# Attention, a Fourier mixer and a gated block on one core: the last row in half-width pairs, the accumulators read ahead of a residual add, the last copies shared otherwise, and a new written order

## The chip, the cores and the metric

The kernel runs on one core of a Trainium2 chip. The core has a matrix engine (TensorE, PE in the rows), a vector engine (VectorE, DVE), an activation engine (ScalarE, ACT), a general engine (GpSimd, POOL), and an engine that issues transfers (SyncE, SP). Each works through its own queue in the order in which its instructions were written; they meet at semaphores. The metric is the time of one execution on the device in microseconds, lower is better.

## The reference

Three stages follow one another. All is float32, with batch 2, 768 positions and 512 channels (8 heads of 64).

```
for each block of 64 positions:                     # decayed linear attention
    out   = ((q k^T) * Dmask) v + (q * lam^(i+1)) state
    state = lam^64 * state + (k * lam^(63-i))^T v
u  = x + real(fft2(x))                              # x: attention output, fft over 768 positions and 512 channels
un = (u - mean(u)) / sqrt(var(u) + 1e-6)
x  = u + relu(un @ w_ch1) @ w_ch2                   # w_ch1 512x2048, w_ch2 2048x512
gate = sigmoid(causal conv of 5 taps over x)
out  = (gate * (x @ w_val)) @ w_out
```

## The kernel before, in words

**Stages.** Each batch element has six chunks of 128 positions for the attention. A chunk `(b, c)` is loaded by `L` (four transfers on SP), gets its scores by `S` (two halves), the mask product on VectorE by `s`, the product with v by `A`, the part from the state by `E`, and the next state by `T` and `t`; `k` and `Kq` scale k and q, `a` and `e` copy the output out of PSUM. `X` moves half of the channels by one partition with transfers on SP. The Fourier stage folds the sequence (`Xm`, `Xe`, `Xo`, `Xx`), transforms the channels (`XD`, with the table cd) and then the positions (`XQ` with the sine table, `XP` with the cosine table), and adds the result into U (`Xc`, `Xq`, `Xp`, `Xu`). Channel 256 of the transform stands alone in one row: `XK` (`fft_P256`, L405) computes it, `XF` (`fft_fix`, L410) puts it into row 0 of the tiles mp. `XA` (`fft_a384`, L335) makes the values that stand for the middle position, for the rows and for channel 256. The step names with a number in front, `0` or `1`, mean the batch.

**Blocks.** After that come four blocks of 384 positions. `Nm` to `Np` are the layer norm; `F` is the first product (16 slices of the hidden width), `f` and `h` its relu as a high and a low part; `G k,f,d` adds slice f into accumulator d (four PSUM banks); `U`, `u`, `V`, `v` split weights into a high and a low part (three products per matmul, `mm3`, L618). In block 0 the first product takes the weights whole. The weights arrive as 64-bit words, and `Dl`, `Da`, `Db`, `Dc`, `De`, `Dx` load and convert them, mostly beside block 0. At a block's end `Rm` (L662) multiplies an accumulator by the reciprocal deviation, and `R` (L666, through `gadd`, L500) adds it to U; `Ha` (L659) gives the next block its four accumulators, which are the same banks, so the first `G` of the next block into bank d waits for `Rm` of d. `M...` is the gated block, one block behind; in the last block `Ev` and `Eo` do its products and `Es` (`end_store`, L686, through `m_store`, L761) copies three tiles of 128 positions out of PSUM and stores them.

**Order.** Nothing is planned at run time: one list, ORDER (L59 to L109), names 1446 steps, and each step is written in that order into its engines' queues. For steps in `GPS` a plus sign behind the step means VectorE and no plus GpSimd; for those in `ACTS` a plus means VectorE and no plus ScalarE. A step that stands later in the list can still run earlier than one on another engine; on one engine the list's order is kept. PSUM tiles with one tag share banks: `pso2` has two, `ph` two, `acc0` to `acc3` one each. U tiles, tables and accumulators are guarded by semaphores that the framework places.

Of the kernel before, what the change touches and what calls it, by code (L numbers as in the profile page):

```python
# [906 lines left out]
```

## Time and profile before

| what | value |
|---|---|
| median of three runs | 451.94 us (450.45 to 452.24) |
| profiled execution, its own time | 451.17 us |
| its span on the core | 449.4 us |
| TensorE busy, share of the span | 438.9 us, 98% |
| VectorE busy | 313.5 us, 70% |
| ScalarE busy | 243.6 us, 54% |
| GpSimd busy | 128.3 us, 29% |
| granted TensorE clock | 1.00 |
| DMA packets | 40.45 MB, mean 90 GB/s |

Busy time is the time in which an engine had at least one instruction at work; matmuls are pipelined, so their ends overlap the next start, and the pace is read from one start to the next. A float32 matmul makes two records in the trace. A row of the timeline gives the start, the time taken, the engine (PEld is the weight load), the line of the kernel, the operation, what it writes and reads, and how many instructions are merged in it; a bracket gives the idle time before it and what ended it.

### The profile page before, as it was taken

How to read it: one execution, taken by the hardware profiler on the slowest of the kernel's cores; microseconds unless marked ns; L12 is line 12 of the kernel's file. 1: busy time of each engine (PE TensorE's matmuls, PEld its weight loads, DVE VectorE, ACT ScalarE, POOL GpSimd, SP SyncE). 2: the span in 40 equal slices, each digit the busy share in tenths (PEclk: the TensorE clock that was granted, in tenths of full speed). 3: DMA queues.
4: the chain of work that ended last, by engine and by line, in shares of the span. 5: the costliest groups of instructions: out<-in, count | busy, mean ns of one | idle time of the engine just before them, and what ended most of it. 6: DMA issues, size and time to landing. Idle time of an engine off the chain costs nothing.

```text
span 449.4 us, 7061 instructions
## 1 busy us (share of the span) xinstructions
PE 438.9 (98%) x2738; PEld 391.8 (87%) x2738; DVE 313.5 (70%) x498; ACT 243.6 (54%) x496; POOL 128.3 (29%) x114
## 2 busy tenths in 40 slices
PE   7999999999999999899999999999999999999996
PEld 6788767678677779899999999999999999999994
DVE  5768789999999998876756478614645893331594
ACT  5454666767767665585426456434634753341442
POOL 1132224101230112343362547232514512330230
PEclk9999999999999999999999999999999999999999
DMA  7999953647733610000000000000000010000101
GB/s 265 327 321 272 393 184 114 207 182 264 269 105 122 224 50 1 1 2 0 1 0 25 0 1 23 1 1 25 1 1 0 25 47 1 0 1 24 48 1 70
DMA packets 15861, 40.45 MB, mean 90 GB/s; under 512 B 2012, under 2 KB 4052, under 8 KB 14804
## 3 DMA queue, kind: packets, MB, share of 16 engines
q1 hardware_dynamic: 15540, 39.62, 25.4%
q8 instruction: 21, 0.34, 0.3%
q10 hardware_dynamic: 288, 0.39, 0.3%
q14 instruction: 12, 0.10, 0.1%
HBM read 35.29 MB, written 3.15 MB: 86 GB/s over the span
## 4 chain that ended last, share of the span: by engine, by line
PE 89%; DVE 5%; DMA 3%; issue 1%; SPq 1%; ACT 0%; DVEq 0%; ACTq 0%
PE acc L622 10%; PE acc L620 10%; PE acc L621 10%; PE ph L628 8%; PE ph L622 8%; PE ph L620 7%; PE ph L621 7%; PE pso L620 4%; PE pso L621 4%; PE pso L622 4%; PE pso L358 2%; PE psS L243 2%; PE pso L258 2%; PE pso L383 2%; PE pso L373 2%; PE pso L269 2%
## 5 line engine op out<-in xcount | busy, mean ns | idle before, releaser
L620 PE MATMUL acc<-g,w2s 128*128 128x384 f32 x240 | 83.6, 348 | 1.3 <-DVE tmp L664 1.3
L622 PE MATMUL acc<-g,w2s 128*128 128x384 f32 x240 | 80.5, 336 | 0.0
L621 PE MATMUL acc<-g,w2s 128*128 128x384 f32 x240 | 80.4, 335 | 0.0
L616 POOL TENSOR_TENSOR w2s<-w,w2s 128x512 fp32r<-128x512 f32 x27 | 36.8, 1363 | 141.8 <-ACT w2s L612 127.2
L612 ACT CAST w2s<-w 128x512 fp32r<-128x512 f32 x62 | 37.9, 618 | 42.9 <-PE acc L622 42.9
L649 DVE SCALAR_TENSOR_TENSOR g<-ph,g 128x384 fp32r<-128x384 f32 x60 | 32.8, 554 | 33.4 <-ACT g L644 33.0
L715 DVE SCALAR_TENSOR_TENSOR gate<-u,cw,gate 128x384 f32<-128x384 f32 (+4 forms) x64 | 48.5, 771 | 1.6 <-ACT gate L710 0.9
L598 ACT CAST w1s<-w 128x512 fp32r<-128x512 f32 x48 | 29.7, 618 | 34.5 <-PE ph L622 34.4
L620 PEld LDWEIGHTS acc<-g,w2s 128*128 128x128 f32 x240 | 45.1, 188 | 3.0 <-DVE tmp L664 1.6
L621 PEld LDWEIGHTS acc<-g,w2s 128*128 128x128 f32 x240 | 45.1, 188 | 1.4
L622 PEld LDWEIGHTS acc<-g,w2s 128*128 128x128 f32 x240 | 45.0, 188 | 0.6 <-DVE w2s L616 0.4
L644 ACT ACTIVATE g<-ph 128x384 fp32r<-128x384 f32 x60 | 29.0, 488 | 28.2 <-PE acc L622 14.7
L620 PE MATMUL ph<-hlA,w1s 128*128 128x384 f32 x128 | 43.4, 339 | 0.6 <-DVE g L649 0.6
L616 DVE TENSOR_TENSOR w2s<-w,w2s 128x512 fp32r<-128x512 f32 x35 | 28.7, 820 | 21.8 <-ACT w2s L612 21.7
L628 PE MATMUL ph<-uc,w 128*128 128x384 f32 x128 | 43.7, 488 | 0.0
L622 PE MATMUL ph<-hlA,w1s 128*128 128x384 f32 x128 | 43.1, 336 | 0.3 <-DVE w1s L602 0.3
L621 PE MATMUL ph<-hlA,w1s 128*128 128x384 f32 x128 | 42.8, 335 | 0.0
L602 POOL TENSOR_TENSOR w1s<-w,w1s 128x512 fp32r<-128x512 f32 x21 | 28.3, 1350 | 50.4 <-ACT w1s L598 35.9
L628 PEld LDWEIGHTS ph<-uc,w 128*128 128x128 f32 x128 | 23.8, 190 | 14.8 <-DVE g L649 0.7
L602 DVE TENSOR_TENSOR w1s<-w,w1s 128x512 fp32r<-128x512 f32 x27 | 23.0, 858 | 18.6 <-ACT w1s L598 18.6
L478 ACT ACTIVATE raw<-raw 128x1024 int32<-128x1024 uint32 (+1 forms) x21 | 23.4, 1118 | 3.4 <-DMA raw<-in_w_dram 2.8
L620 PEld LDWEIGHTS ph<-hlA,w1s 128*128 128x128 f32 x128 | 24.0, 188 | 1.3 <-DVE g L649 0.9
(206 smaller groups left out, 947.1 us busy)
## 6 DMA issues: line engine op xcount, KB each, us to landing
raw<-in_w_dram SPq DMA_DIRECT2D x16, 1024.0 KB, 4.9
ldqk<-in_qT_dram SPq DMA_DIRECT2D x12, 256.0 KB, 5.2
ldqk<-in_k_dram SPq DMA_DIRECT2D x12, 256.0 KB, 5.4
...
```

Source lines behind the costliest of these rows:

```text
L478: self.nc.scalar.activation(w, w.bitcast(U32), AF.Copy, bias=-0.5 + 2.0 ** -17, scale=2.0 ** -29 - 2.0 ** -47)
L598: self.nc.scalar.copy(w[:, 0], self.raw1(f))
L602: eng.tensor_tensor(w[:, 1], self.raw1(f), w[:, 0].bitcast(F32), op=ALU.subtract)
L612: self.nc.scalar.copy(w[:, 0], self.raw2(f))
L616: eng.tensor_tensor(w[:, 1], self.raw2(f), w[:, 0].bitcast(F32), op=ALU.subtract)
L620: nc.tensor.matmul(out, lh, rh, start=start, stop=False)
L621: nc.tensor.matmul(out, lh, rl, start=False, stop=False)
L622: nc.tensor.matmul(out, ll, rh, start=False, stop=stop)
L628: self.nc.tensor.matmul(ph, self.raw1(f)[:, t], self.uc[k][:, t], start=(t == 0), stop=(t == 3))
L644: self.nc.scalar.activation(g[:, 0], self.ph[(k, f)], AF.Relu)
L649: self.nc.vector.scalar_tensor_tensor(g[:, 1], self.ph[(k, f)], 0.0, g[:, 0].bitcast(F32), op0=ALU.max, op1=ALU.subtract)
L715: self.nc.vector.scalar_tensor_tensor(gp[:, o:TB], x, w, gp[:, o:TB], op0=ALU.mult, op1=ALU.add)
```

## The change

Five edits. `fft_P256` computes its row as two matmuls of half the columns each (every second column, 64 weight columns), one into partitions 0 to 63 and one into 64 to 127, in place of one over all 385 columns with 128 weight columns; `fft_fix` reads row 0 and row 64 accordingly; and `fft_a384` takes one column of the table, repeated, as the weights of its third group, so that its value stands in all rows, and copies three values in one instruction in place of two instructions. `end_store` copies tile 1 in two halves on two engines and tile 2 whole on ScalarE, in place of the other way round, and `m_store` gives the first half to VectorE and SP and the second to ScalarE and its queue. ORDER has a new order of steps up to the first part of block 1 (its first 700 steps), with the four `Rm` of block 0 ahead of its residual adds. In the whole list 149 steps change the engine: plus signs come and go. Up to the middle of block 1, 39 steps go from VectorE to GpSimd and 21 the other way; from there on 28 and 40, with the order the same but for those signs. A few copies of the attention and the transform change between ScalarE and VectorE.

The new list in the parts that the text speaks of, and the code:

```diff
-S0,0,0 S0,0,1 L0,1 s0,0,0 s0,0,1 Kl A0,0 k0,0,0 k0,0,1 L0,2 T0,0 Kq0,1+ e0,0+ k0,1,0 S0,1,0 S0,1,1 t0,0 k0,1,1 T0,1 Y0,1 s0,1,0 L0,3 Xcs1 s0,1,1 A0,1 a0,0 Kq0,2+ t0,1 k0,2,0 S0,2,0
-S0,2,1 Y0,2 E0,1 k0,2,1 s0,2,0 L0,5 T0,2 s0,2,1 a0,1 Kq0,3+ A0,2 k0,3,0 e0,1+ t0,2 S0,3,0 Y0,3+ S0,3,1 k0,3,1 T0,3 L0,4 s0,3,0 S0,5,0 s0,3,1 A0,3 t0,3 Y0,4+ S0,5,1 E0,2 s0,5,0 L1,0 E0,3
...
-Rm0,1 G0,15,0 u1,3+ G0,14,3 Rm0,0 G0,15,3 R0,1 R0,0+ F1,2 V1,0 f1,0 v1,0+ Mg0,0 h1,0 G0,15,2 Mg0,1 wv3+ F1,3 f1,2 Rm0,2 h1,2 V1,1 v1,1+ U1,6 R0,2+ Rm0,3 Ha1 G1,0,0 G1,0,3 U1,4 G1,0,1
...
-Eo2,1 My3,3 Mk3,3+ Eo3,0 Eo3,2 Es0 Eo3,1 Es2 Es1
+S0,0,0 S0,0,1 k0,0,0 Kl s0,0,0 k0,0,1 s0,0,1 L0,1 k0,1,0 T0,0 L0,2 t0,0 k0,1,1 S0,1,0 A0,0 S0,1,1 k0,2,0 Kq0,1+ Kq0,2 a0,0+ L0,3 s0,1,0 s0,1,1 k0,2,1 T0,1 S0,2,0 Y0,1 k0,3,0 e0,0+ S0,2,1
+s0,2,0 A0,1 E0,1 t0,1 S0,3,0 Y0,2 s0,2,1 S0,3,1 T0,2 a0,1+ e0,1 Kq0,3+ L0,5 k0,3,1 s0,3,0 s0,3,1 A0,2 t0,2 E0,2 S0,5,0 S0,5,1 L0,4 T0,3 Y0,3+ e0,2+ k0,4,0 s0,5,0 s0,5,1 t0,3 A0,3 a0,2+ L1,0
...
+Xo0,0,0+ Xo0,1,0+ E1,1 T1,2 A1,2 e1,1+ E1,2 XA0 Xo0,0,1 Xx0 XD0,2,0 Xo0,1,1 Dl0 Xcs0 XD0,0,0 S1,3,0 Xcs1 S1,3,1 Y1,2+ Xd0,0,0 t1,2 Xd0,2,0+ Da0 XD0,1,1 XD0,1,0 Xd0,1,0 Xd0,1,1+ e1,2+ L1,4
+XD0,2,1 Dx0 k1,3,0 XD0,0,1 Xd0,2,1+ Db0 Kq1,3 Dl1 Xd0,0,1 Dc0 XP0,1 XQ0,1 a1,1 k1,3,1 Xc0,1 Kq1,4+ Xq0,1 XP0,0 s1,3,0 XQ0,0 S1,4,0 s1,3,1 Xq0,0 Xp0,1,1+ Xp0,1,0 S1,4,1 De0 XK0 Da1 X1,0
...
+h1,1 Da16 Na1,3+ G0,15,3 h1,0 G0,15,2 wo1 V1,0 Rm0,0 F1,2 G0,15,1 v1,0 Rm0,2 u1,4+ U1,3 V1,2 Rm0,3 Rm0,1 u1,3 Ha1 Dl18 G1,0,2 G1,0,0 Da18 G1,0,3 Db16 f1,2 h1,2 De20 Nv1 G1,0,1 F1,4 v1,2+
+Db18 V1,1 Dx16 R0,0 Nw1 F1,3 Dc16 v1,1 G1,1,1 G1,1,0 U1,5 Dx18 u1,5+ G1,1,3 U1,6 G1,1,2 G1,2,1 G1,2,3 f1,3 h1,3 De16 Dc18 V1,3 f1,4 Mg0,0 De18 u1,6+ Wv0 Wv1 Wv2 G1,2,0 h1,4 F1,5 F1,6 U1,7
...
+Es0 Eo3,1 Es2 Es1
@@ -337,15 +336,14 @@
         cd, z = self.cd, self.PM[b]
         ps = self.ps_o.tile([P, 512], F32, name="pso2", tag="pso2")
         for g in range(3):
-            x = [(cd[:, a, g * P:(g + 1) * P], z[:, 0, a, HS:HS + 1]) for a in range(2)]
+            x = [(cd[:, a, g * P:(g + 1) * P] if g < 2 else cd[:, a, 256:257].to_broadcast([P, P]), z[:, 0, a, HS:HS + 1]) for a in range(2)]
             if g < 2:
                 x.append((self.odd, z[:, 1, 0, HS:HS + 1]))
             for n, (w, y) in enumerate(x):
                 nc.tensor.matmul(ps[:, g * P:(g + 1) * P], w, y.to_broadcast([P, P]), start=(n == 0), stop=(n == len(x) - 1))
         a384 = self.a384[b] = f.tile([P, 2, 3], F32, name="a384", tag="a384", bufs=2)
         for w in range(2):
-            nc.scalar.activation(a384[:, w, 0:2], ps[:, 0:2 * P:P], AF.Copy, scale=1.0 - 2.0 * w)
-            nc.scalar.activation(a384[0:1, w, 2:3], ps[0:1, 2 * P:2 * P + 1], AF.Copy, scale=1.0 - 2.0 * w)
+            nc.scalar.activation(a384[:, w], ps[:, 0:3 * P:P], AF.Copy, scale=1.0 - 2.0 * w)
 
     def fft_D(self, b, j, w):
         nc = self.nc
@@ -405,14 +403,21 @@
     def fft_P256(self, b):
         ps = self.p256[b] = self.ps_o.tile([P, 512], F32, name="pso2", tag="pso2")
         for j in range(3):
-            self.nc.tensor.matmul(ps[:, 0:HS + 1], self.AB[b][:, j, 256:384], self.cs[0][:, j, :], start=(j == 0), stop=(j == 2))
+            for x in range(2):
+                self.nc.tensor.matmul(
+                    ps[64 * x:64 * x + 64, 0:HS // 2 + 1 - x], self.AB[b][:, j, 256:320], self.cs[0][:, j, x:HS + 1:2],
+                    start=(j == 0), stop=(j == 2), skip_group_check=True,
+                )
 
     def fft_fix(self, b):
 
         n = HS + 1
         for w in range(2):
             for x in range(2):
-                self.nc.scalar.activation(self.mp[(b, 0, w)][0:1, x:n:2], self.p256[b][0:1, x:n:2], AF.Identity, bias=self.a384[b][0:1, x, 2:3])
+                r = slice(64 * x, 64 * x + 1)
+                self.nc.scalar.activation(
+                    self.mp[(b, 0, w)][0:1, x:n:2], self.p256[b][r, 0:HS // 2 + 1 - x], AF.Identity, bias=self.a384[b][r, x, 2:3]
+                )
 
 
     def cv_units(self):
@@ -684,7 +689,7 @@
         self.mm3(self.oend[t], self.gvr[k][:, 0, e, ts_], self.gvr[k][:, 1, e, ts_], self.wo[:, 0, e], self.wo[:, 1, e], e == 0, e == 3)
 
     def end_store(self, t):
-        self.m_store(NBLK - 1, t, self.oend[t], (self.nc.scalar.copy, self.nc.vector.tensor_copy, None)[t])
+        self.m_store(NBLK - 1, t, self.oend[t], (self.nc.scalar.copy, None, self.nc.scalar.copy)[t])
 
 
     def m_split(self, k, d):
@@ -766,7 +771,7 @@
             o = self.p3.tile([P, DM], F32, name="o", tag="o", bufs=2)
         r0 = hf * TB + t * P
         if copy is None:
-            for eng, q, c in ((self.nc.scalar.copy, self.nc.scalar, 0), (self.nc.vector.tensor_copy, self.nc.sync, 256)):
+            for eng, q, c in ((self.nc.vector.tensor_copy, self.nc.sync, 0), (self.nc.scalar.copy, self.nc.scalar, 256)):
                 eng(o[:, c:c + 256], ps[:, c:c + 256])
                 q.dma_start(self.out[b, r0:r0 + P, c:c + 256], o[:, c:c + 256])
             return
```

## Rows read from the trace of the kernel before

**Rows 1.** the page, totals: busy us, share of the span, instructions of each engine.

```profile
PE 438.9 (98%) x2738; PEld 391.8 (87%) x2738; DVE 313.5 (70%) x498; ACT 243.6 (54%) x496; POOL 128.3 (29%) x114
```

**Rows 2.** windows: us; busy PE, PEld, DVE, ACT, POOL; PEclk; DMA share; GB/s.

```profile
6.00:40.00 34.00, 32.13 (x512) 27.52 (x512) 26.82 (x52) 19.14 (x74) 6.60 (x9) 1.00 0.94 319
40.00:165.00 125.00, 123.75 (x675) 91.80 (x672) 112.92 (x162) 84.71 (x153) 24.39 (x21) 1.00 0.58 202
165.00:200.00 35.00, 33.06 (x190) 32.42 (x189) 28.53 (x46) 21.64 (x43) 10.08 (x8) 1.00 0.00 1
```

**Rows 3.** waits of TensorE: us in total, times, longest.

```profile
PE pso L258 <- DVE pa L249: 1.3, 3, 1.0
PE acc L620 <- DVE tmp L664: 1.3, 1, 1.3
...
PE pso L344 <- DMA cd<-in_cd_dram: 1.0, 1, 1.0
PE ph L620 <- DVE g L649: 0.6, 1, 0.6
PE ph L622 <- DVE w1s L602: 0.5, 2, 0.3
PE psS L243 <- DMA ldkT<-in_kT_dram: 0.3, 1, 0.3
```

**Rows 4.** timeline of TensorE around the last row of batch 0.

```profile
58.82 1.09 PE L258 MATMUL pso<-pa,ldv 128*64 128x128 f32 x16
59.84 1.09 PE L269 MATMUL pso<-qs,st 64*64 64x128 f32 x16
...
62.91 2.10 PE L408 MATMUL pso<-cos,AB 128*128 128x385 f32 x6
64.95 1.09 PE L258 MATMUL pso<-pa,ldv 128*64 128x128 f32 x16
```

**Rows 5.** timeline of VectorE, GpSimd and TensorE at the turn to block 1.

```profile
179.38 1.64 DVE L501 TENSOR_TENSOR u<-u,tmp 128x384 f32<-128x384 f32 x1
180.94 0.55 DVE L664 TENSOR_TENSOR tmp<-acc,rstd 128x384 f32<-128x384 f32 x1
...
179.26 2.89 POOL L602 TENSOR_TENSOR w1s<-w,w1s 128x512 fp32r<-128x512 f32 x2 [4.24 <-ACT w1s L598]
...
181.54 0.44 PE L620 MATMUL acc<-g,w2s 128*128 128x384 f32 x1 [1.31 <-DVE tmp L664]
```

**Rows 6.** groups of instructions, VectorE: count, busy us, mean ns, idle before.

```profile
L616 DVE TENSOR_TENSOR w2s<-w,w2s 128x512 fp32r<-128x512 f32 x35 | 28.7, 820 | 21.8 <-ACT w2s L612 21.7
```

**Rows 7.** timeline of VectorE, GpSimd and TensorE near 158 us.

```profile
158.05 1.76 DVE L602 TENSOR_TENSOR w1s<-w,w1s 128x512 fp32r<-128x512 f32 x1
...
157.94 1.32 POOL L501 TENSOR_TENSOR wo<-wf,wo 128x512 fp32r<-128x512 f32 x1 [10.26 <-ACT wo L491]
...
159.86 0.45 PE L622 MATMUL ph<-hlA,w1s 128*128 128x384 f32 x1 [0.25 <-DVE w1s L602]
```

**Rows 8.** timeline of the tail: ScalarE, VectorE, SyncE's queue.

```profile
444.94 0.37 ACT L770 COPY gate<-acc 128x256 f32<-128x256 f32 x1
...
445.34 0.42 DVE L770 COPY gate<-acc 128x256 f32<-128x256 f32 x1 [2.02 <-ACT gate L770]
445.69 0.68 DVE L773 COPY o<-acc 128x512 f32<-128x512 f32 x1
...
446.39 0.33 SPq L774 DMA_DIRECT2D out_dram<-o  x1
```

**Rows 9.** timeline of VectorE at the start.

```profile
8.72 1.36 DVE L188 TENSOR_TENSOR_SCAN lampow<-lam_hc,tmp 128x128 f32<-128x128 f32 x4
```

**Rows 10.** SyncE's queue: issues of the tables; last row: KB and us to landing.

```profile
10.82 0.43 SPq L183 DMA_DIRECT2D sin<-in_sin_dram  x1
...
40.04 0.43 SPq L183 DMA_DIRECT2D cos<-in_cos_dram  x1
...
cos<-in_cos_dram SPq DMA_DIRECT2D x1, 577.5 KB, 9.5
```

More of the change, by code (lines that the diff above doesn't have):

```diff
@@ new lines @@
+G0,9,0 Dx17 Xu1,1,1+ De11 Xu1,2,1 Na1,1 v0,12+ Xu1,3,0+ I Nh1,3 Dl15 Na1,2+ F0,14 Da17 f0,11 V0,11 h0,11 f0,14 Dl19 Da15 h0,14 G0,12,2 G0,12,0 F0,10 u1,1 G0,12,3 G0,12,1 Da19 Db15 Db17
+v0,11+ Dx15 G0,11,1 V0,10 f0,10 Db19 G0,11,0 v0,10 G0,11,2 F0,13 Dc17 h0,10 Nl1,3 G0,11,3 Dc15 G0,10,3 G0,10,1 De17 F1,1 G0,10,2 G0,10,0 f0,13 h0,13 Nq1,3 Wo0 V0,13 De15 V0,14 Dx19 v0,14
+U1,0 Dl20 F0,15 G0,14,3 f0,15 u1,0 v0,13+ Dl16 G0,14,1 G0,13,0 Da20 Dc19 h0,15 Wo1 G0,13,2 G0,13,3 G0,14,0 Db20 G0,13,1 F1,0 f1,1 De19 V0,15 G0,14,2 v0,15+ Dx20 Dc20 f1,0 G0,15,0 wo0 U1,4
@@ new lines @@
+G1,4,3 wv3 f1,5 G1,4,1 U1,8 G1,4,0 Mg0,2 V1,5 G1,4,2 h1,5 Mz0,0 F1,10 u1,8 v1,5 f1,7 Mz0,1 Ml0,0 Mz0,2 h1,7 V1,8 Ns3,1 F1,8 Ml0,2+ U1,9 Mt0,1,2 u1,9+ Ms0,0 Mz0,3 v1,8+ Wo3 Ml0,1+ G1,5,3
+G1,5,1 U1,11 G1,5,0 G1,5,2 Ml0,3+ u1,11+ Np1 Mt0,3,2 Mv0,2 f1,10 V1,6 h1,10 F1,9 v1,6+ Mt0,3,1 Mt0,3,0 Mt0,2,3 Ms0,3 G1,6,0 Mt0,2,2 G1,6,3 U1,14 Mt0,2,1 G1,6,2 Mt0,2,0 G1,6,1 Mv0,3 u1,14
+Ms0,2 f1,8 h1,8 V1,7 Mt0,1,1 F1,11 Mx0,3 Ns2,1+ v1,7+ Ns3,0+ Mx0,2 Mv0,0 Ns3,2+ Mt0,1,0 U1,12 Ms0,1 u1,12 G1,7,3 Mx0,0 G1,7,0 G1,7,1 My0,0 Mk0,0 G1,7,2 My0,3 G1,8,3 f1,9 Mk0,3+ G1,8,2 h1,9
@@ new lines @@
+v3,0+ F3,0 f2,15 U3,7 h2,15 G2,15,0 u3,7+ G2,15,3 U3,12 G2,15,1 Rm2,0 G2,15,2 Rm2,1 F3,7 f3,0 Rm2,3 V3,2 R2,3+ h3,0 Nv3 u3,12 v3,2+ F3,12 U3,2 Rm2,2 Ha3 Mx1,3 R2,1+ My1,3 R2,0 u3,2 G3,0,0
+Mg2,1 Nw3 G3,0,3 U3,3 G3,0,2 G3,0,1 Mg2,0 f3,7 Mk1,3+ Mo1,0 Mt2,1,3 V3,1 Mz2,0 h3,7 Mz2,1 v3,1 Mt2,1,2 Mz2,3 F3,2 Me1,0 Mt2,1,1 R2,2+ u3,3+ G3,1,3 G3,1,2 Mg2,2 G3,1,1 Mt2,0,3 Ml2,0 U3,11
+G3,1,0 Mt2,0,2 Mo1,1 Mz2,2 V3,3 f3,2 h3,2 v3,3+ Mg2,3 Mt2,0,1 F3,3 Mt2,0,0 Ml2,1+ Mt2,2,3 Ms2,0 G3,2,3 Mt2,2,2 G3,2,2 U3,4 Mt2,1,0 G3,2,1 Mt2,2,1 G3,2,0 Ms2,1 u3,11+ Mo1,2 V3,6 u3,4 f3,3
@@ new lines @@
+v3,6 h3,3 Mt2,2,0 F3,4 Nd3+ Ms2,2 Me1,2 Me1,1 G3,3,3 Ml2,2 G3,3,2 U3,8 Ml2,3 G3,3,1 Mt2,3,3 G3,3,0 Mt2,3,2 u3,8+ Mv2,0 Mt2,3,1 V3,4 f3,4 Mv2,1 v3,4+ h3,4 Mx2,0 Mt2,3,0 My2,0 G3,4,0 Ms2,3
+G3,4,1 Mx2,1 G3,4,3 Mk2,0 My2,1 G3,4,2 F3,8 Mk2,1 V3,5 v3,5 G3,5,2 G3,5,3 f3,8 G3,5,0 U3,6 h3,8 G3,5,1 Mv2,2 u3,6+ V3,7 v3,7+ Mv2,3 Mx2,2 My2,2 F3,6 Mk2,2 f3,12 h3,12 Mx2,3 F3,11 f3,6 U3,9
+h3,6 My2,3 G3,6,0 u3,9+ G3,6,1 U3,14 G3,6,2 Mk2,3 u3,14 G3,7,1 G3,7,2 G3,7,0 G3,6,3 F3,9 V3,11 f3,11 v3,11+ h3,11 G3,7,3 F3,14 V3,8 f3,9 U3,10 h3,9 v3,8 G3,8,0 G3,8,1 f3,14 G3,8,3 U3,13
@@ new lines @@
+h3,14 u3,10 Np3 F3,10 u3,13 F3,13 U3,15 u3,15+ G3,8,2 f3,13 Mo2,0 V3,9 h3,13 f3,10 v3,9 h3,10 G3,9,0 G3,9,1 Me2,0 G3,9,3 G3,9,2 Mo2,1 V3,10 v3,10 G3,10,0 G3,10,3 G3,10,1 G3,11,0 G3,11,1
+G3,11,3 G3,10,2 G3,11,2 Mo2,2 V3,13 V3,12 v3,13+ v3,12+ F3,15 V3,14 V3,15 v3,14 Me2,2 G3,12,0 v3,15+ f3,15 G3,13,0 G3,14,0 Me2,1 h3,15 G3,15,0 G3,12,1 G3,13,1 Rm3,0 G3,14,1 R3,0+ G3,15,1
+Mz3,0 G3,12,2 Mg3,0 G3,13,2 Rm3,1 Ml3,0 G3,14,2 R3,1+ G3,15,2 Mt3,0,3 Mz3,1 G3,12,3 Rm3,2 Mg3,1 G3,13,3 Ml3,1 G3,14,3 Mt3,1,3 G3,15,3 Mt3,1,2 Ev0,0 Ev1,0 R3,2+ Ev0,1 Mt3,0,2 Mz3,2 Ev2,0
```

71 lines of the change are left out of this document (26 added, 45 removed).

## The prediction

> **What bounds the kernel now.** I read the totals first: TensorE is busy 438.9 of 449.4 us, VectorE 70%, ScalarE 54%, GpSimd 29% [rows 1]. Then the table by stage: VectorE works 112.92 of the 125 us from 40 to 165 us, TensorE 123.75, and in the first 34 us behind 6 us the DMA engines are 0.94 busy [rows 2]. Third, the list of what TensorE waited for: six waits of 0.3 to 1.3 us, 5.0 us in all [rows 3]. So time leaves in three ways only: less TensorE work, fewer of these waits, or a shorter tail. Work moved off VectorE or ScalarE gives nothing by itself; it counts where it ends one of the waits or starts a new one. The granted clock is 1.00 in every stretch [rows 2], so the clock has no part in it.
>
> The sum is made against the profiled execution: 451.17 us, a span of 449.4 and 1.8 around it. It lies 0.8 us under the median of the three times, 451.94.
>
> **Last row in pairs (XK).** Before, three matmuls of 385 columns (two records each) run per batch: six records from 62.91 to the next group at 64.95, 2.04 us, 0.34 a record [rows 4]. After, each is two of 193 and 192 columns with 64 weight columns, into partitions 0 to 63 and 64 to 127. The nearest thing shown is the same shape in attention: 16 records with 64 weight columns and 128 moving ones take 58.82 to 59.84, 1.02 us, so 127 ns a pair, where one alone of 128 columns at 0.84 ns a column (323 ns over 385) would take 107 [rows 4]: the two halves of the array run side by side at some 20 ns a pair extra. A pair of 193 is then 162 + 20 = 182 ns, six of them 1.09, and about 0.1 for the change of shape that the 2.04 also holds. Gain 0.86 a batch, 1.7 us in all, every bit on TensorE. Bounds: no gain, if the halves run one after another or the every-second-column read is slower (no row shows one), and 2.0 if the 20 ns vanishes. I take 1.7, nearest to the row. The a384 matmuls keep their count; a weight read that repeats one column is not shown, so the four matmuls concerned (eight records) might double at the most, 8 x 128 columns x 0.84 ns = 0.9 us [rows 4], or lose nothing; I take 0, since only the load differs and loads lie beside matmuls (the loads' own row in the totals adds 391.8 us under the same 438.9 [rows 1]). Two tiny ScalarE instructions fewer a batch are hidden, ScalarE having idle time throughout [rows 1].
>
> **Accumulator ahead of the residual add.** At the turn from block 0 to block 1 TensorE waits 1.31 us for the last `Rm` product at 180.94, because the add R0,2 stands before it on VectorE and took 1.64 us instead of about 0.55 beside a GpSimd op that started at 179.26 [rows 5]. In the new list all four Rm stand ahead of `Ha1`, no R0 between them, and between the last accumulation G0,15,1 and the matmul that needs that bank (G1,0,1) lie three other groups of three (some 1.6 us) against one split and two products on VectorE (0.8 + 2 x 0.55 [rows 5, 6], the first of them beside G0,15,1). What is late next is v1,0, now on GpSimd behind wo0 and wo1: three ops of 1.3 us [rows 7], some 4 us, which F1,0, F1,2 and four groups (over 6 us) cover; if GpSimd came 3 us late, that cover is gone. I take the whole 1.3; bounds +0.5 to -1.3.
>
> **Tail.** Now the last copy is one VectorE op of 128x512, 0.68 us from 445.69, then SP's issue at 446.39 [rows 8]. After it is halved: VectorE 0.42 and ScalarE 0.37 (both durations from the halves of tile 2) side by side, each with its own queue. ScalarE first does tile 2 whole; its half copy starts at 444.94 now, so a whole one, some 0.65 by VectorE's ratio of whole to half, ends at 445.6, before 445.69. Gain 0.26 plus perhaps 0.1 for the smaller transfer: 0.3. Bounds 0 to 0.5.
>
> **The new order.** 1: `Kl` (four scans, 1.36 us [rows 9]) now stands before the first two mask products on VectorE. Behind it wait s0,0,0 and s0,0,1, and behind those A0,0 and S0,1 (its bank). T0,0, some 0.6 us (16 records of half the width of rows 4), and half of S0,1 fill part of the gap: I take +0.3 net of what TensorE waited there before (1.3 in three waits [rows 3]), bounds -1.0 to +1.3. 2: the sin table (577.5 KB) leaves its place at 10.82 on SP, where the DMA engines are full, for one right behind the cos table [rows 10]. At 319 GB/s that is 1.8 us less ahead of the later chunks: the 0.3 wait for kT goes (-0.3). cd lands earlier by up to as much, and T1,2 now stands ahead of the matmuls that need it: of that 1.0 wait I take -0.7 (0 to -1.0). 3: SP's queue: L1,3 and the first weight load stay ahead of both tables; sin then stands behind cos, which took 9.5 us from issue at 40.04 [rows 10], and lands some 2 us later, about 51.5. TensorE needs it after the DFT's column part and XP0,1, by my walk near 52: cost 0, with about 0.5 to spare. 4: up to the middle of block 1, 39 small ops go from VectorE to GpSimd and 21 come back: 18 net, at 0.55 to 0.8 us each some 11 us off VectorE, at about 1.2 us each some 21 us onto GpSimd (1.32 against 0.82 for a 128x512 split [rows 6, 7]). The 0.25 us wait behind the stretched w1s op at 158.05 [rows 7] goes (-0.2). Later, 28 go one way and 40 the other, with TensorE fed throughout: 0. 5: most of block 0's conversions and splits move by some positions; from 40 to 165 us TensorE idled 1.25 us in all, 1.0 for cd and 0.25 for w1s [rows 2, 3, 7], so there is nothing else to win and a wait can come. VectorE ended waits of 3.7 us in the whole run [rows 3]; for a new list I allow two of the size of the 0.6 one: +1.2, bounds 0 to +4.
>
> One row speaks against item 4: the op at 158.05 took 1.76 us while the GpSimd op from 157.94 ran 1.32 [rows 7], and R0,2 likewise [rows 5]. The Trainium skill, SBUF — State Buffer, section Terms, says that VectorE and GpSimd share one port pair, held by one of them for a whole instruction while the other stands still. The trace agrees where it can be seen: the GpSimd op ends at 159.26, and the VectorE op 0.55 later, at 159.81. By that rule the 21 us may hold VectorE for as long, which is rival 2 below.
>
> **The sum.** -1.7 - 1.3 - 0.3 + 0.3 - 0.3 - 0.7 - 0.2 + 1.2 = -3.0: 451.17 - 3.0 = 448.2 us.
>
> **Rivals.** 1, the pairs don't run side by side: six pairs cost the old 2.04 or a little more, 449.9 us. For it: every second column has no row; against it: the attention pairs do [rows 4]. Chance 0.08, half of it under 449.7.
>
> 2, VectorE behind GpSimd. Up to 200 us TensorE lost 1.31 + 0.25 behind VectorE ops that GpSimd stretched [rows 5, 7], with 41 us of GpSimd work from 6 to 200 us [rows 2]; 21 more make 0.8 at that rate. If the accumulator wait also stays, since another add or split is stretched there, the time is 448.2 + 1.3 + 0.8 + 0.2 = 450.5, and with one more such wait at LN or the first splits 452. Against it: VectorE itself has 11 us less to do. Chance 0.20.
>
> 3, slower: the tables come late. If L1,3 or the weight loads hold SP so that sin is issued or served behind the next chunk and weight loads (1 MB each, 3.3 us at 319 GB/s), it lands near 58 instead of 51.5. XQ0,1 stands in TensorE's queue, and LN, all of block 0 and the end move with it: 6 to 7 us, 454 to 455. It decides from a landing 6 us after TensorE is ready. For it: the DMA engines are 0.94 full just before and cos took 9.5 us; against it: sin directly follows cos on the same queue. The long rearranged stretch has other chains of that kind. Chance 0.10.
>
> 4, the list packs better than I allow: none of the 1.2 comes and the head's wait goes too: 448.2 - 1.2 - 1.0 = 446.0. Chance 0.07.
>
> **How the numbers follow.** The forecast has 0.55, its own range 446.5 to 449.7. Under 0.5% (2.3 us of 451.94) is about what a measurement cannot tell from no change: faster is under 449.7, slower over 454.2. Faster: 0.53 of the forecast, 0.04 of rival 1, 0.07 of rival 4: 0.64. Slower: 0.10 of rival 3, 0.02 of rival 2. Same: the remaining 0.24. The range reaches from rival 4 less its bound, 445.5, up to rival 2's 452, which leaves rival 3 and the edges out, less than 0.2.
>
> **What would show it.** The twelve records of the last row as 24 in 2 x about 1.1 us, partitions 64 on; no wait of TensorE on an Rm product near 175 us; the last two copies side by side at the end; no wait for kT or cd; VectorE's busy time between 40 and 165 us down by some 10 us and GpSimd's up by about 20. Wrong would be: records of 0.16 us one behind another; a wait of over 1 us for sin near 52 us; waits of TensorE on g, w1s or u in block 0 adding up to more than 1.2 us.

## The result, and the profile after

The changed kernel takes 453.97 us (median of 11 runs, 452.98 to 458.19) against 451.94 for the kernel before: a ratio of 1.0059, interval 1.0038 to 1.008. It is slower by about 0.6%; 448.2 was predicted. Its profiled execution took 454.65 us with a span of 452.9, so against the one of before (span 449.4) it lost 3.5 us, and that is the difference that the traces have to explain.

The totals and the list of waits say where to look (busy us, share, instructions; then engine, line, waited for: us in total, times, longest), the changed kernel:

```profile
PE 438.7 (97%) x2750; PEld 392.6 (87%) x2750; DVE 314.5 (69%) x494; ACT 239.1 (53%) x488; POOL 146.7 (32%) x120
```

```profile
PE ph L625 <- DVE g L654: 3.5, 2, 2.2
PE pso L356 <- DVE var L563: 1.9, 1, 1.9
...
PE psS L242 <- DMA ldkT<-in_kT_dram: 1.1, 1, 1.1
PE psS L242 <- DVE pa L248: 0.9, 1, 0.9
PE pso L257 <- DVE pa L248: 0.6, 1, 0.6
PE ph L633 <- DVE uc L534: 0.6, 1, 0.6
PE psd L301 <- ACT kd L228: 0.2, 1, 0.2
```

The waits shown of before [rows 3] that were to go are gone: no `Rm` product (1.3), no cd (1.0), no w1s (0.5). But the sum is 8.8 us where it was 5.0 [rows 3, with the one for `onesr` ahead of the work left out on both sides]. The prediction had it 1.0 lower. And the clock, which was 1.00 in every stretch [rows 2], isn't any more. From 40 to 165 us VectorE is as busy as before (112.47 us; 112.92 [rows 2]), though GpSimd works 20 us more there; the prediction expected VectorE some 10 us lower. The windows of the changed kernel (us; busy PE, PEld, DVE, ACT, POOL; PEclk, DMA share, GB/s):

```profile
6.00:40.00 34.00, 31.74 (x480) 27.48 (x481) 23.51 (x48) 18.35 (x71) 8.76 (x9) 0.95 0.92 304
40.00:165.00 125.00, 121.86 (x712) 92.24 (x711) 112.47 (x145) 77.53 (x140) 44.84 (x31) 1.00 0.56 194
...
32.00:34.00 2.00, 1.13 (x11) 1.16 (x13) 1.65 (x4) 1.89 (x8) 0.29 (x2) 0.74 0.90 336
34.00:36.00 2.00, 2.00 (x19) 1.78 (x18) 1.51 (x3) 0.13 (x1) 0.00 (x0) 0.50 1.01 298
36.00:38.00 2.00, 2.00 (x42) 1.83 (x39) 1.14 (x3) 1.33 (x6) 0.00 (x0) 0.90 0.93 231
```

**The books.** Three things change the span: TensorE's waits, TensorE's work, and the clock. The waits grew by 3.8 us. The work shrank by the two last rows in pairs; the one of batch 0 lasts 1.09 us where it was 2.04 (below), and twice that is taken: -1.9. From 32 to 38 us a granted clock of 0.74, 0.50 and 0.90 takes 0.26, 0.50 and 0.10 of 2 us each: +1.7. Sum: 449.4 + 3.8 - 1.9 + 1.7 = 453.0; the span is 452.9. The row of batch 1 gained less: from its start to the second product behind it there are 1.47 us (134.47 to 135.94) where there were 2.12 (126.58 to 128.70), 0.65 in place of 0.95. So -1.9 may be 0.3 too much; no reading below hangs on that.

**Where TensorE stood.** Its rows with an idle time (in brackets, with what ended it), the changed kernel:

```profile
31.49 0.46 PE L242 MATMUL psS<-ldqk,ldkT 64*128 64x128 f32 x2 [1.06 <-DMA ldkT<-in_kT_dram]
32.87 1.94 PE L242 MATMUL psS<-ldqk,ldkT 64*128 64x128 f32 x14 [0.92 <-DVE pa L248]
...
92.48 1.13 PE L356 MATMUL pso<-cd,F 128*128 128x256 f32 x4 [1.89 <-DVE var L563]
...
193.97 0.45 PE L625 MATMUL ph<-hlA,w1s 128*128 128x384 f32 x1 [2.25 <-DVE g L654]
199.64 0.44 PE L625 MATMUL ph<-hlA,w1s 128*128 128x384 f32 x1 [1.21 <-DVE g L654]
```

Four places, and at three of them VectorE is the one that comes late. What stood ahead on VectorE, and what GpSimd did beside it:

```profile
89.23 3.12 DVE L491 SCALAR_TENSOR_TENSOR w<-raw,w 128x1024 int32<-128x1024 int32 x1
92.28 0.15 DVE L563 TENSOR_SCALAR var<-pso 128x3 f32<-128x3 f32 x1
...
190.54 1.23 DVE L491 SCALAR_TENSOR_TENSOR wf<-raw,wf 128x1024 int32<-128x1024 int32 x1
191.69 1.76 DVE L607 TENSOR_TENSOR w1s<-w,w1s 128x512 fp32r<-128x512 f32 x1
193.37 0.55 DVE L654 SCALAR_TENSOR_TENSOR g<-ph,g 128x384 fp32r<-128x384 f32 x1
...
197.21 1.90 DVE L720 SCALAR_TENSOR_TENSOR gate<-u,cw,gate 128x382 f32<-128x382 f32 x3
```

```profile
88.21 1.84 POOL L332 TENSOR_TENSOR F<-pm 1x384 f32<-1x384 f32 x1 [3.31 <-DVE F L328]
90.02 1.25 POOL L621 TENSOR_TENSOR w2s<-w,w2s 128x512 fp32r<-128x512 f32 x1
...
191.21 4.93 POOL L506 TENSOR_TENSOR wvr<-hlB,wvr 128x512 fp32r<-128x512 f32 x3 [4.38 <-ACT wvr L729]
```

At 92 us the next matmuls of the channel transform (`XD`) need the `pso2` bank that `Nv0` filled, and the bank is free once `Nw0` has read it (92.28). `Nw0` stands in the list behind `De3`, a conversion that took 3.12 us beside two GpSimd ops; the same kind of op took 1.21 at 85.24. At 194 and 200 the relu halves `h1,4` and `h1,6` stand behind the conversion of w_out and a split of 1.76 us, and behind three gate taps. That split runs beside three GpSimd ops (191.21 to 196.14); another of its kind took 0.68 at 196.61. At 31 and 33 us the head's second chunk of batch 1 comes too early for its load, and then for VectorE, on which `Kq1,1` had waited 4.62 us for another part of the same load, ahead of the mask products.

### The profile page after: what moved, and what is told of

It reads as the page before. It is cut to its first block, busy times and chain, and to the rows that moved or that the text cites. A ratio compares the mean times of both kernels' runs of the same rounds, so it can differ in the third digit from the quotient of the medians.

```text
span 452.9 us, 7082 instructions
## 1 busy us (share of the span) xinstructions
PE 438.7 (97%) x2750; PEld 392.6 (87%) x2750; DVE 314.5 (69%) x494; ACT 239.1 (53%) x488; POOL 146.7 (32%) x120
## 4 chain that ended last, share of the span: by engine, by line
PE 83%; DVE 10%; ACT 2%; issue 2%; DMA 2%; SPq 1%; DVEq 0%; ACTq 0%
PE acc L627 10%; PE acc L625 10%; PE acc L626 10%; PE ph L633 8%; PE ph L625 7%; PE ph L626 7%; PE ph L627 7%; PE pso L627 4%; PE pso L625 4%; PE pso L626 4%; PE pso L356 2%; PE psS L242 2%; PE pso L371 2%; PE pso L381 2%; PE pso L257 1%
## 5 line engine op out<-in xcount | busy, mean ns | idle before, releaser
L621 POOL TENSOR_TENSOR w2s<-w,w2s 128x512 fp32r<-128x512 f32 x25 | 34.7, 1387 | 100.6 <-ACT w2s L617 92.4
L621 DVE TENSOR_TENSOR w2s<-w,w2s 128x512 fp32r<-128x512 f32 x37 | 31.5, 858 | 24.7 <-ACT w2s L617 24.7
L720 DVE SCALAR_TENSOR_TENSOR gate<-u,cw,gate 128x384 f32<-128x384 f32 (+4 forms) x64 | 43.9, 699 | 1.0 <-ACT gate L715 0.3
L607 DVE TENSOR_TENSOR w1s<-w,w1s 128x512 fp32r<-128x512 f32 x28 | 21.4, 763 | 16.3 <-ACT w1s L603 16.2
L228 ACT ACTIVATE kd<-ldqk,mask 128x64 f32<-128x64 f32 x80 | 20.4, 335 | 10.9 <-DMA ldqk<-in_k_dram 9.0
```

Source lines behind the costliest of these rows:

```text
L228: self.nc.scalar.activation(kt[:, h // 2, h % 2], kn[:, h // 2, h % 2], AF.Copy, scale=dec[:, h % 2, h // 2])
L607: eng.tensor_tensor(w[:, 1], self.raw1(f), w[:, 0].bitcast(F32), op=ALU.subtract)
L621: eng.tensor_tensor(w[:, 1], self.raw2(f), w[:, 0].bitcast(F32), op=ALU.subtract)
L720: self.nc.vector.scalar_tensor_tensor(gp[:, o:TB], x, w, gp[:, o:TB], op0=ALU.mult, op1=ALU.add)
```

## The experiments

Two theories stood against each other at first. By one the loss is GpSimd's: steps given to it by the new signs stretch VectorE's ops or come late themselves. By the other it is the order on VectorE's queue: what TensorE waits for stands behind long ops. The expectations below call the first theory G and the second theory O. A third came up on the way: the amount of VectorE work that the list puts into one stretch (theory load). "New code" is the pairs, `fft_a384` and the tail. The books of every run, in us: waits without `onesr`; clock = the sum of 2 us times the part not granted in the stretches of 2 us below 0.97; "sum" = 449.4 + (waits - 5.0) - 1.9 where the pairs are in + clock.

| kernel | ratio to before, interval | waits | clock | sum | span |
|---|---|---|---|---|---|
| changed kernel | 1.0059 (1.0038 to 1.0080) | 8.8 | 1.7 | 453.0 | 452.9 |
| code_only | 1.0002 (0.9983 to 1.0021) | 6.6 | 0 | 449.1 | 449.1 |
| after_signs_before | 1.0108 (1.0087 to 1.0130) | 9.1 | 5.1 | 456.7 | 455.9 |
| before_signs_after | 1.0173 (1.0152 to 1.0194) | 13.7 | 0 | 456.2 | 457.9 |
| head_after_rest_before | 1.0014 (0.9994 to 1.0034) | 7.5 | 0 | 450.0 | 449.5 |
| head_before_rest_after | 1.0081 (1.0058 to 1.0105) | 11.0 | 0 | 453.5 | 453.9 |
| after_o_fix | 1.0028 (1.0010 to 1.0047) | 6.4 | 1.7 | 450.6 | 450.0 |
| after_g_fix | 1.0123 (1.0093 to 1.0154) | 9.4 | 3.4 | 455.3 | 454.1 |
| after_o_fix2 | 1.0027 (1.0002 to 1.0052) | 7.2 | 1.7 | 451.4 | 452.0 |
| after_o_fix2_load | 0.9996 (0.9981 to 1.0011) | 7.0 | 0 | 449.5 | 450.1 |
| fix_less | 0.9947 (0.9928 to 0.9966) | 4.5 | 0 | 447.0 | 447.4 |
| code_rm_tail | 0.9974 (0.9956 to 0.9992) | 5.9 | 0 | 448.4 | 448.1 |
| code_rm_db | 0.9983 (0.9962 to 1.0004) | 6.6 | 1.7 | 450.8 | 451.2 |
| rm_only | 0.9966 (0.9950 to 0.9981) | 3.5 | 0 | 447.9 | 448.4 |
| rm_late | 1.0053 (1.0033 to 1.0073) | 6.5 | 1.7 | 452.6 | 452.9 |

The sum meets the span within 0.8 us in 13 of 15 rows (1.2 and 1.7 off in the other two), so these three terms are where the time is. In after_signs_before and after_g_fix the low clock began while TensorE still stood (at about 91.5 of a wait to 93.11, and 90.7 of one to 91.92), so some 0.8 and 0.6 us are counted in both terms there; without that they come to 455.9 and 454.7. The 1.7 of before_signs_after stays open. The clock term is summed up to 208 us. The spans are of one execution; the ratios are of medians, in which the clock's part varies. It is no accident of one execution, though: the mean granted clock was 0.996 or less in 10 of the 11 executions of the changed kernel, and 0.998 or more in 71 of the 95 of the one before that ran beside the experiments.

**The code without the list.** The old list with the old signs, all code edits:

```diff
 ORDER = """   # as before
+fft_P256, fft_fix, fft_a384, end_store, m_store as in the change
```

> The list of before, with its plus signs, and only the code of the change: the row in pairs, the shorter a384, the last copies shared otherwise. Theory G (the loss of the change comes from GpSimd ops standing in VectorE's way) and theory O (it comes from the order: what stands ahead of what on the queues) both expect the pairs' gain here alone, 2 x 0.85 us, and nothing from the tail, where the second half copy waited for the first: 450.2 us where before has 451.9, ratio 0.996. If the pairs gave nothing, 451.9.

No change: 1.0002. Its TensorE rows at the last row of batch 0, and VectorE's beside them:

```profile
62.87 1.25 PE L409 MATMUL pso<-cos,AB 128*64 128x193 f32 x12
63.96 1.04 PE L259 MATMUL pso<-pa,ldv 128*64 128x128 f32 x16
...
67.45 1.09 PE L270 MATMUL pso<-qs,st 64*64 64x128 f32 x16 [0.90 <-DVE qs L218]
```

```profile
65.96 1.44 DVE L218 TENSOR_TENSOR qs<-ldqk,lampow 128x512 f32<-128x512 f32 x1
...
65.85 0.99 POOL L508 TENSOR_TENSOR tmp<-u 128x384 f32<-128x384 f32 x1 [8.59 <-DVE u L508]
```

The same VectorE op in the kernel before, and TensorE behind the last row of batch 1 in code_only:

```profile
66.89 0.68 DVE L217 TENSOR_TENSOR qs<-ldqk,lampow 128x512 f32<-128x512 f32 x1
```

```profile
128.81 0.44 PE L629 MATMUL acc<-g,w2s 128*128 128x384 f32 x1 [0.54 <-DVE w2s L623]
```

The row lasts 1.09 us from its start to the next group (62.87 to 63.96), where before it lasted 2.04 [rows 4]. The pairs do run side by side. But 3.5 us later TensorE stands 0.90 us for a VectorE op that no edit touches, and that wait was not there before. The op came 0.93 us earlier than before, and so fell beside a GpSimd add that it had missed (65.85 to 66.84 here, 65.99 to 67.00 before): it took 1.44 us in place of 0.68. Behind the last row of batch 1 TensorE stands 0.54 us, also new, for a split that took as long as before (1.15 us; 1.12). Of the 1.6 us by which the whole run's waits grew, 1.4 are these two, and they ate most of the gain. Both theories had expected 0.996.

**Which half of the new list: signs or order.** The new order with each step's old engine, and the old order with the new engines (both with the new code):

```diff
-... De3 Nw0 Db5 Xx1 XD1,0,0 ...    # changed kernel: Xx1 on GpSimd
+... De3 Nw0 Db5 Xx1+ XD1,0,0 ...   # after_signs_before: every sign as before
```

> The changed kernel in its new order, with every step on the engine that it had before. Theory G: the waits of TensorE near 90, 191 and 198 us (1.9, 2.2 and 1.2) go, since the GpSimd ops beside the stretched VectorE ops go: 450 us, ratio to before about 0.996. Theory O: the order keeps its waits and VectorE has 11 us more to do: 454 to 457 us, ratio 1.005 to 1.012.

> The order of before with the new code and every step on the engine of the changed kernel. Theory G: slower than the code alone by 2 to 4 us, 452 to 454 us, ratio 1.000 to 1.005. Theory O: as the code alone, 450 us, 0.996.

Both are worse than the change as a whole, 1.0108 and 1.0173. So neither half alone is the fault: signs and order fit each other. The first meets theory O's number; the second was expected by neither theory (1.005 was theory G's most). With the old signs the stretching is less, and still the time is longer. The window of that kernel, in the same columns as above:

```profile
40.00:165.00 125.00, 120.58 (x690) 90.44 (x689) 103.53 (x151) 76.55 (x139) 26.26 (x20) 0.97 0.56 192
```

VectorE is busy 103.53 us there with 151 instructions, against 112.47 with 145 in the changed kernel, where GpSimd does 44.84 us in place of 26.26. Fewer instructions took 9 us longer. The two windows don't hold quite the same steps, since this kernel is 3.5 us behind at the last row of batch 1; counted from 40 us to that row, VectorE is busy 84.75 us with 114 instructions in the changed kernel and 80.14 with 118 here, and GpSimd 30.84 and 22.51. That is rival 2's mechanism, at some half a microsecond of VectorE for each one of GpSimd (8.9 for 18.6, or 4.6 for 8.3). The Trainium skill, SBUF — State Buffer, section Terms, has the two engines share one port pair that one of them holds for a whole instruction; the two windows agree with it in the direction. The waits for g near block 1 fell with the old signs, too, from 3.5 to 1.1 us in all, as theory G has it (a wait of 1.6 us for an accumulator product came in). What cost this run its time was one step in the wrong place of a queue: `Xx1`, a one-row op back on VectorE, behind a conversion, the eight small ops of `Nw0` and a clamp. TensorE, then VectorE:

```profile
93.11 0.79 PE L360 MATMUL pso<-odd,F 128*128 128x128 f32 x2 [3.66 <-DVE F L334]
```

```profile
88.51 1.78 DVE L493 SCALAR_TENSOR_TENSOR w<-raw,w 128x1024 int32<-128x1024 int32 x1
...
92.52 0.54 DVE L334 TENSOR_TENSOR F<-pm 1x384 f32<-1x384 f32 x1
```

That wait and the low clock that came with it (3.4 of the 5.1 us, 0.8 of them inside the wait) make 6.3 us, of the 6.5 by which the span is longer than that of the kernel before. `Xx1` left on GpSimd with the other old signs was not run, so what the signs alone would give in the new order is open; TensorE's long stop also gave VectorE time to catch up.

**Which part of the list.** Cut at the first product of block 0 (F0,0): the new list to there and the old one's order behind it, and the reverse.

```diff
 ORDER = new list up to F0,0, then the steps left, as the old list has them   # head_after_rest_before
 ORDER = old list up to F0,0, then the steps left, as the new list has them   # head_before_rest_after
```

> The new list up to the first product of block 0 (step F0,0), then the remaining steps in the order and on the engines of before. TensorE came to that product at 73.23 us in the changed kernel against 73.47 before, so if the loss lies behind it (both theories, in the part from 73 to 200 us), this is the code alone plus some 0.7: 451 us, ratio 0.998. If the head leaves VectorE a backlog that costs later, 453 or more, 1.003.

> The list of before up to the first product of block 0, then the remaining steps in the order and on the engines of the changed kernel: the mirror of the last run, which took 451.9 us. If the whole loss lies behind F0,0 (waits of 1.9 near 90 us and 2.2 and 1.2 near 191 and 198), this has it: 454 us, ratio 1.005. If the two halves of the list only lose together, 452, ratio 1.000.

1.0014 and 1.0081, where 0.998 and 1.005 had been named for a loss behind F0,0. Both are higher, but the loss is there: behind it the second run has the waits of 1.9 and 3.5 that the changed kernel has.

**The three places, by order or by engine.** On the changed kernel, either three steps moved ahead of what they stood behind, or the GpSimd ops beside them given to VectorE:

```diff
-... Dc3 f0,3 De3 Nw0 ... Mg0,0 De18 u1,6+ Wv0 Wv1 Wv2 G1,2,0 h1,4 ... Mt0,0,2 ... G1,3,0 h1,6 ...
+... Dc3 f0,3 Nw0 De3 ... Mg0,0 h1,4 De18 u1,6+ Wv0 Wv1 Wv2 G1,2,0 ... h1,6 Mt0,0,2 ... G1,3,0 ...   # after_o_fix
...
-... Nw0 Db5 Xx1 ... wv1 ... wv0 ... wv3 ...
+... Nw0 Db5 Xx1+ ... wv1+ ... wv0+ ... wv3+ ...   # after_g_fix
```

> The changed kernel with three steps moved on VectorE's queue, no step on another engine: Nw0 ahead of De3, h1,4 ahead of De18 and of the split u1,6, h1,6 ahead of three gate taps. Theory O (what stands ahead of what on VectorE): the three waits of TensorE (1.9, 2.2, 1.2) shrink to under 0.4 each, 454.0 - 4.5 = 449.5 us, ratio 0.995. Theory G (the time that GpSimd ops take from VectorE is missing whatever the order): the stretched ops stay, and the time comes back at the next step that waits: 452.5 us or more, ratio over 1.001.

> The changed kernel in its own order with four ops taken back from GpSimd to VectorE: the one-row add Xx1 (1.84 us beside the 3.12 us op that TensorE waited for near 90) and the three wv splits beside the 1.76 us op near 191. Theory G: the stretched ops near 90 and 191 take their own 1.2 and 0.7 us, the waits shrink by 1.2 and 1.0: 451.7 us, ratio 1.000. Theory O: VectorE has 2.6 us more in the same places, and the waits stay or grow: 454 to 456 us, ratio 1.005 or more.

The moves take back half, 1.0028; the engines make it worse, 1.0123, again by `Xx1`. But that does not decide for order over engine. In after_g_fix the two stretched ops ran at their own pace and the waits behind them shrank as theory G had it: `De3` took 1.23 us and the wait for `Nw0` (1.89) is gone; the split took 0.68, and the wait behind it is 1.17 where it was 2.25. What was lost is `Xx1`, now in VectorE's queue behind the eight small ops of `Nw0` and a clamp, 4.33 us, with 3.4 us of clock in the table beside it. So the time meets theory O's expectation, and the rows meet theory G's. The rows of after_g_fix, TensorE and then VectorE:

```profile
91.92 0.79 PE L360 MATMUL pso<-odd,F 128*128 128x128 f32 x2 [4.33 <-DVE F L334]
195.20 0.45 PE L627 MATMUL ph<-hlA,w1s 128*128 128x384 f32 x1 [1.17 <-DVE g L656]
```

```profile
87.87 1.23 DVE L493 SCALAR_TENSOR_TENSOR w<-raw,w 128x1024 int32<-128x1024 int32 x1
...
194.00 0.68 DVE L609 TENSOR_TENSOR w1s<-w,w1s 128x512 fp32r<-128x512 f32 x1
```

With the moves the wait at 92 us is gone and the one at 200 is down to 0.16, so order alone is enough there. But a new wait stands at 191 us in after_o_fix, for the split `u1,6` behind `De18`, and the time is what theory G had named for this run (452.5 us or more, the time coming back at the next step):

```profile
191.06 0.45 PE L629 MATMUL ph<-hlA,w1s 128*128 128x384 f32 x1 [1.75 <-DVE w1s L609]
```

**Chasing the wait, and the head.** u1,6 moved too; and then, on top, the load of the head's chunk earlier and its `Kq` behind the mask products:

```diff
-... A0,4 X0,0 S1,0,1 L1,1 E0,4 Kq1,1+ k1,0,1 ... s1,0,1 S1,1,0 ... h1,4 De18 u1,6+ Wv0 ...
+... A0,4 X0,0 S1,0,1 L1,1 E0,4 Kq1,1+ k1,0,1 ... s1,0,1 S1,1,0 ... h1,4 u1,6+ De18 Wv0 ...   # after_o_fix2
+... A0,4 L1,1 X0,0 S1,0,1 E0,4 k1,0,1 ... s1,0,1 Kq1,1+ S1,1,0 ... h1,4 u1,6+ De18 Wv0 ...   # after_o_fix2_load
```

> The order fix of the changed kernel (ratio 1.0028), in which a new wait of 1.8 us for the split u1,6 at 189 us had come, since it still stood behind the two long conversions De18 and Dc18; now u1,6 goes ahead of De18 as well. Theory O: the 1.8 us wait goes, 452.9 - 1.6 = 451.2 us, ratio 0.999. Theory G: VectorE is short of time in this stretch, the next step waits as long: 452.5 us or more, ratio over 1.002.

> The same, and near 30 us the four transfers of chunk (1,1) ahead of the shift X0,0 on SyncE's queue, and the scaling Kq1,1, which held VectorE for 4.6 us until its load came, behind the mask products s1,0. Theory O: the two waits there (1.0 for kT, 1.2 for the mask product) shrink by 1.5 together, and TensorE's low clock behind them is not seen: 449.7 us, ratio 0.9955. If the head's gain is taken back at the next load or by VectorE: 451, ratio 0.999.

The first wins nothing (1.0027), again as theory G had it: the wait comes back behind the next ops. The second reaches 0.9996; its head has neither the wait for kT nor the one behind it, and the granted clock is 1.00 from 28 to 40 us. What it keeps, near block 1 (with 0.67 us more at 195.12):

```profile
192.95 0.45 PE L629 MATMUL acc<-g,w2s 128*128 128x384 f32 x1 [1.37 <-DVE w2s L623]
...
201.82 0.45 PE L627 MATMUL ph<-hlA,w1s 128*128 128x384 f32 x1 [1.72 <-DVE g L656]
```

**Order of single steps or amount of work.** In fix_less the clamp, shift and sign of weight unit 18 (half of w_out) are left out of the kernel above, so that its w_out is not the reference's. In rm_late the old list with its `Rm0,3` moved (rm_only, below) gets the clamp and shift of the same unit later; the work is the same.

```diff
 def cv_clamp(self, u):      # and cv_shift, cv_sign: fix_less
+    if u == 18:
+        return
...
-... G0,12,2 Db18 G0,13,3 ... V0,15 Dc18 f1,1 ... Mg0,2 De18 ...
+... G0,12,2 G0,13,3 ... V0,15 f1,1 ... Mg0,2 Db18 Dc18 De18 ...   # rm_late
```

> The new code and list with the five moves of the version before (Nw0, h1,4, h1,6, u1,6 and the head's load), and with one conversion left out on VectorE: the clamp, shift and sign of unit 18 (the second half of w_out), whose three ops took 1.51, 1.22 and 2.32 us at 181, 186 and 188 us. The output then holds a wrong w_out. Theory load (VectorE has too much work between 178 and 205 us because the list brings conversions there): the waits at 192.95 (1.37), 195.12 (0.67) and after 201 (1.7) shrink to under 1.2 in all, and the time falls by some 2.5 us to 449.5 (ratio 0.994 to 0.997). Theory order (what TensorE waits for stands behind other long ops): the waits stay over 2.5 in all at the gate's taps, and the ratio stays between 0.998 and 1.001.

> The kernel before with Rm0,3 ahead of R0,0 (0.9966 alone), and with the clamp and the shift of the same unit 18 (0.69 and 1.22 us, at 165.6 and 168.9) moved behind the turn to block 1, right ahead of its sign op near 189 us. The work is the same. Theory load: 1.9 us more on VectorE between 180 and 192, where it is 0.8 to 0.95 busy, bring waits of TensorE of 1 to 2 us there, ratio 0.999 to 1.001. Theory order: g, w1s and w2s of that stretch stand ahead of them or far enough ahead of their matmuls, no new wait over 0.3 us, ratio 0.9966 within 0.001.

Taking the work out gives 0.9947, 0.5% under the same list with it, and one wait of 1.68 us remains of 3.8 us between 190 and 203; under 1.2 was expected. It stands behind a gate tap that took 1.63 us beside a GpSimd split (0.61 for the tap before it). In fix_less, TensorE and VectorE:

```profile
198.92 0.45 PE L633 MATMUL ph<-hlA,w1s 128*128 128x384 f32 x1 [1.68 <-DVE g L662]
```

```profile
196.76 1.63 DVE L728 SCALAR_TENSOR_TENSOR gate<-u,cw,gate 128x383 f32<-128x383 f32 x1
```

Putting 1.9 us of work into the same stretch of the old list costs from 0.9966 to 1.0053, nearly 4 us, twice the work; 0.999 to 1.001 was expected of it. In rm_late TensorE and its clock in one window of 1 us, then VectorE and GpSimd:

```profile
198.47 0.69 PE L621 MATMUL ph<-hlA,w1s 128*128 128x384 f32 x1 [3.24 <-DVE g L650]
198.95 0.52 PE L622 MATMUL ph<-hlA,w1s 128*128 128x384 f32 x1
199.27 0.52 PE L623 MATMUL ph<-hlA,w1s 128*128 128x384 f32 x1
```

```profile
199.00:200.00 1.00, 1.00 (x5) 1.00 (x4) 1.00 (x3) 1.00 (x4) 0.00 (x0) 0.50 0.00 0
```

```profile
192.22 1.78 DVE L502 TENSOR_TENSOR wvr<-hlB,wvr 128x512 fp32r<-128x512 f32 x1
...
191.45 2.01 POOL L603 TENSOR_TENSOR w1s<-w,w1s 128x512 fp32r<-128x512 f32 x1 [7.04 <-ACT w1s L599]
```

A wait of 3.24 us (0.6 in rm_only), and behind it matmuls 320 ns apart where they were 175. The books of the twofold price: 1.9 us moved in; a split behind it that came late enough to fall beside a GpSimd op and took 1.78 us, where it takes 0.69 in rm_only; and 1.7 us of clock. The amount of VectorE work counts, then: from 180 to 200 us it is busy 18.7 of 20 us in the changed kernel, 15.9 in the one before. But these two runs don't part amount from place, since the ops taken out or put in also stand in front of the relu half that TensorE waits for. What speaks for the amount is the pair of after_o_fix2 and fix_less: moving steps only moved the wait, taking work out removed most of it.

**The accumulators alone, and the tail.** Before's code and list with one step moved; the same with the new code and the two half copies of the tail in two separate tiles; and that list with a clamp (Db1) moved behind the scaling qs, with the new code.

```diff
-... Rm0,0 G0,15,3 R0,1 R0,0+ ... U1,6 R0,2+ Rm0,3 Ha1 ...
+... Rm0,0 G0,15,3 R0,1 Rm0,3 R0,0+ ... U1,6 R0,2+ Ha1 ...   # rm_only, code_rm_tail, code_rm_db
...
+    o2 = self.const.tile([P, 512], F32, name="gate", tag="gate1", bufs=2)   # code_rm_tail: second half copied to o2
...
-... XK0 Db1 Xq0,0 ... Xu0,2,0 Nm0 ...
+... XK0 Xq0,0 ... Xu0,2,0 Db1 Nm0 ...   # code_rm_db
```

> The kernel before, its old code and list, with one step moved: Rm0,3 ahead of R0,0 and R0,2. Both theories: the 1.3 us wait near 181 goes, 450.3 us, ratio 0.997. With the code of the change it was 0.9974; if the pairs' gain is wholly given back this is the same, if it shows once the wait is gone this is 0.999.

> The list of before with the new code and one step moved: Rm0,3 ahead of the residual adds R0,0 and R0,2 on VectorE; and the last copy's second half in a tile of its own. The accumulator wait of 1.3 us near 181 goes; the two last copies start together. The code alone gave 451.9 us: both theories expect 451.9 - 1.3 - 0.3 = 450.3 us, ratio 0.9965. If VectorE sets the pace there as it did where the pairs' gain was given back (a 0.9 us wait for qs), the wait moves to the next product and the ratio stays 0.999 to 1.000.

> The list of before with the new code, Rm0,3 moved, and one conversion step of 0.7 us (Db1) moved on VectorE's queue from ahead of the scaling qs that TensorE waited 0.9 us for near 66 us to behind the mask products. Theory O: that wait falls to 0.2 and the pairs' gain in batch 0 shows: 450.5 - 0.7 = 449.8 us, ratio 0.9957. If VectorE has no time to spare from 60 to 165 us, the 0.7 comes back behind it: ratio 0.9974 as before.

rm_only is the fastest here of the kernels that do all the work: 449.92 us, 0.9966, ahead of the kernel before and of the changed one. Its list of waits has no accumulator; the longest of it:

```profile
PE pso L345 <- DMA cd<-in_cd_dram: 1.1, 1, 1.1
PE pso L259 <- DVE pa L250: 1.1, 3, 0.8
...
```

code_rm_tail has the pairs on top and is no faster (0.9974): its waits are 5.9 against 3.5. The pairs show no gain here even with that wait gone; the intervals leave room for some 0.7 us of it. Moving the clamp is undecided (0.9983, its interval reaches from below rm_only's to no change); the wait for `qs` of 0.9 us stayed, so the clamp was not what held it: qs took 1.44 us there too, beside the same GpSimd add. The tail, VectorE and ScalarE, of the changed kernel and then of code_rm_tail:

```profile
449.12 0.42 DVE L775 COPY o<-acc 128x256 f32<-128x256 f32 x1 [2.27 <-PE acc L627]
...
449.58 0.37 ACT L775 COPY o<-acc 128x256 f32<-128x256 f32 x1 [0.51 <-DVE o L775]
```

```profile
444.43 0.42 DVE L778 COPY o<-acc 128x256 f32<-128x256 f32 x1 [2.27 <-PE acc L629]
...
444.95 0.37 ACT L778 COPY gate<-acc 128x256 f32<-128x256 f32 x1 [0.58 <-DVE o L778]
```

The two halves run one behind the other, 0.79 us, also into separate tiles. What they still share is the PSUM tile that both read; whether the framework's semaphore or the chip sets this order wasn't tried.

## Why the prediction was wrong

**The pairs** (-1.7): right as a cost, -1.6 to -1.9; wrong in "every bit on TensorE". From 40 to 165 us VectorE is busy nine tenths [rows 2], and TensorE came earlier to points that VectorE sets. In code_only two new waits, 0.90 and 0.54, stand right behind the two rows. The row for VectorE was read for its total; at which hand-overs it would then be late was not asked.

**The accumulators** (-1.3): right. Moved alone it gives 0.34%, 1.5 us of 451.61.

**The tail** (-0.3): wrong, 0. From its last copy's start to the end of the span the changed kernel takes 3.8 us (449.12 to 452.9), the one before 3.7 [rows 8]. The row that said so was there: in [rows 8] the second half copy idles 2.02 us until the first is over, on another engine.

**The head** (kT -0.3, cd -0.7, Kl +0.3): cd went. TensorE had no wait at the first mask products, where the kernel before had 1.3 and the sum allowed 0.3 more, but came so early to the next chunk that it waited 1.06 for its kT and 0.92 behind it, and the clock fell: 1.7 us for which the prediction had no term. Head and rest together cost what the list of waits says; where the gain of one passes into the other can't be read from one mark, since steps changed sides of it.

**New waits** (+1.2, bounds 0 to +4): this is the step that failed. "I allow two of the size of the 0.6 one" took the old list's waits as a measure of the new one's. The sum left 4.0 us of waits; they come to 8.8. 5.4 of them are in three places, 1.9, 2.25 and 1.21, all of one kind: a short VectorE op that frees TensorE stands behind long ones, of 1.2 to 3.1 us. Three things make it late, and each shows in a run: its place in the queue (after_o_fix, half of the loss back); GpSimd, which stretches the ops ahead of it (after_g_fix: the waits of 1.89 and 2.25 fell to none and 1.17); and the amount of VectorE work between 180 and 203 us (fix_less after after_o_fix2). How the loss divides among the three is open, since no run changes one of them alone.

**Rival 2** named the mechanism that stretches the ops (3.12 for 1.21, 1.76 for 0.68), and with it item 4 of the new order failed: VectorE's work did not fall by the 11 us moved off it, 313.5 before, 314.5 after. It gave 450.5 to 452, since it priced a stretched op by the rate of the old list. Rival 3 (tables late) did not come; its time, 454 to 455, was met by another way. Giving four steps back to VectorE as after_g_fix did is no cure, because `Xx1` then came late; the three splits without `Xx1`, on top of the moves of after_o_fix, were not tried.
